# A two-layer FNet and PEER kernel: score weights made from two pieces of w_q at a time, and four smaller moves of buffers and order

## The chip, the cores and the metric

The kernel runs on one core of one Trainium2 chip. The metric is the device time of one execution in microseconds (us); a run's number is the time of that core. Five engines work side by side, each with its own instruction stream: PE (matrix multiply; PEld is its weight load), DVE (elementwise work and reductions), ACT (activations and copies), POOL (here one power per tile) and SP, whose stream issues the DMAs. The engines meet only at semaphores.

## The reference

The input x has 2048 rows of 512 numbers. Two sublayers alternate, twice each, and each adds its result to x:

```python
def A(x):                       # Fourier mixing, real part
    a, b = x @ dft_hid_re.T, x @ dft_hid_im.T
    return dft_seq_re @ a - dft_seq_im @ b
def B(x):                       # PEER: 32 heads, 16 + 16 keys, 256 experts, top 2 of the pairs
    q = einsum("nd,dhc->nhc", x, w_q)            # w_q: 512 x 32 x 256
    s1, s2 = q[..., :128] @ k1.T, q[..., 128:] @ k2.T      # 16 scores each
    ... top 2 of s1, top 2 of s2, top 2 of their four sums, softmax g ...
    act = gelu(einsum("nd,nhkd->nhk", x, u[top_e]))
    return einsum("nhk,nhk,nhkd->nd", g, act, v[top_e])
x = x + A(layernorm(x)); x = x + B(layernorm(x))
x = x + A(layernorm(x)); x = x + B(layernorm(x))
```

## The kernel before

**Numbers in two parts.** Every operand of a large matmul is split into a high part (rounded to the PE's fp32r) and a low part (the rest): xh and xl for the normalized x, ch and cl for a piece C of the sequence DFT matrix, dh and dl for the hidden DFT, wh and wl for the scores. A product is three matmuls: high by high, high by low, low by high.

**Setup.** w_q is never multiplied by x. The scores are linear in x, so k1 and k2 are first multiplied into w_q, which gives wh and wl (512 x 2 x 32 x 16). w_q comes in 32 loads of 512 KB (two heads each, tile wr). For each one DVE splits it into three bf16 pieces (line 381, f1, and line 384, f2, tile w), PE does 24 small matmuls of 48 columns against the keys (line 392, f3), DVE adds up the three pieces (line 397, f4, tile ws), ACT writes wh (line 404) and DVE wl (line 407). One such group on PE is called a visit here. The hidden DFT, u and v come through wr too and are split (lines 324 to 332).

**Sequence DFT.** `seq_unit` does the sequence DFT of one block of 256 rows (the last 256 rows: two of 128): for each of 16 row tiles s of x a piece C is loaded (line 454, tile raw, four buffers), ACT rounds it to ch (line 458), DVE makes cl (line 462), and PE adds 12 matmuls of 512 columns into four PSUM accumulators acc (line 518; lines 498 and 503 for the first s tiles). ACT and DVE then take acc out as pth and ptl (lines 543 and 546).

**Row tiles.** `token_tile` takes 128 rows through the rest: the second (hidden) DFT on pth and ptl (line 615, f), the addition of x (line 625), layer norm (lines 245 to 263, 271), a transpose (line 664), scores (lines 694 and 698, copied by ACT to tile sc, line 703), the product with u (line 725) and its gelu on act (lines 730 to 745), the top-2 chain on DVE (lines 778 to 894), a transpose of the choice (lines 903 and 907, tile qt), one-hot masks on DVE (lines 926 and 932, tile lr), mask matmuls (line 943), the copy of their diagonal by ACT (line 955), which goes out to DRAM and back as gt (line 999 and after), the weights times act (line 1014), a transpose (line 1023, then ph and pl, lines 1027 and 1031), the product with v (lines 1044 and 1048) and the addition to x (line 1064). The very last row tile, called fine, takes the diagonal by matmuls (line 978, weighed at line 1012) instead of the DRAM way.

**The order.** Every step is an `Op` with an engine, a planned cost, what it comes after, what buffers (`Hold`) it takes and gives back, and a priority. `Plan.run` places all of them once, by planned costs, when the kernel is built; each engine then executes its stream strictly in that order. `behind` is a constraint on the order alone. Buffers are counted in `BUFS`. While PE waits for the first data it runs ten matmuls without use (`FILL0`), and others are put in planned gaps at the end.

**The start.** x comes in 16 loads of 256 KB (line 297), the C pieces between them. For the first `FIRST` tiles ACT makes xh straight from x and a second full-precision copy for xl (both line 271), and the PE work of one tile is f (8 matmuls with xh) and g (4 with xl).

The buffers and the diagonal's copy as they stand:

```python
BUFS = {"acc": 4, "bank": 4, "raw": 4, "c": 3, "p": 1, "row": 4, "wr": 5, "wp": 2,
        "tok": 3, "sc": 1, ..., "lr": 4, ...}
...
hgs, hbs = Hold("p" if spare_p else "sc"), [Hold("bank") for _ in range(2)]
...
t["gs"] = work([P, 16, 4, E], F32, "sc") if not spare_p else mixed()...
```

Of the kernel before, what the change touches and what calls it, by code (L numbers as in the profile page):

```python
# [8 lines left out]
F32 = mybir.dt.float32  # L9
# [15 lines left out]
SP = 1  # L25
# [19 lines left out]
FIRST = 4  # L45
# [115 lines left out]
def load(kb):  # L161
    return kb / 256 * 1.05
# [3 lines left out]
def spectral_peer_kernel(ctx: ExitStack, tc, x_in, cseq, ctile, dhid, wq, k1t, k2t, ut, vm, out):  # L166
# [9 lines left out]
    BUFS = {"acc": 4, "bank": 4, "raw": 4, "c": 3, "p": 1, "row": 4, "wr": 5, "wp": 2,  # L176
            "tok": 3, "sc": 1, "eq": 1, "act": 3, "q": 2, "top": 1, "qt": 1, "lr": 4, "gt": 1, "pp": 1, "gdr": 2, "bn": 1}
# [19 lines left out]
    half = const.tile([P, 1], F32, name="half")  # L197
    picks = const.tile([P, P], F32, name="picks")

# [40 lines left out]
    def ln_stats(get, i, after, prio):  # L240
        bn, h = {}, Hold("bn")

        def f0():
            bn[0] = apool.tile([P, 6], F32, name="bn", bufs=BUFS["bn"])
            nc.vector.bn_stats(bn[0], get())

        a = op("DVE", dve(512), f0, after, take=[h], prio=prio)
        return ln_rest(lambda: bn[0], h, i, [a], prio)

    def ln_rest(bn, h, i, after, prio):  # L250
# [14 lines left out]
        a = op("DVE", 0.1, f1, after, last=[h], prio=prio)  # L265
        a = op("DVE", 0.1, f2, [a], prio=prio)
        a = op("POOL", 0.5, f3, [a], prio=prio)
        return op("DVE", 0.1, f4, [a], prio=prio)
# [9 lines left out]
    def xhat(layer, i, get, after, take, last, prio):  # L278
        if layer == 0 and i < FIRST:
# [3 lines left out]
                                  [a], last=last, prio=prio)  # L283
# [6 lines left out]
    xload = {}  # L290
    for i in range(NT):
        def first(i=i):
            h, t = Hold("wr"), {}

            def f():
                t[0] = setup_pool().tile([P, D], F32, name="wr", bufs=BUFS["wr"])
                nc.sync.dma_start(t[0], x_in[i * P:(i + 1) * P, :])
# [3 lines left out]
            a = ln_stats(lambda: t[0], i, [a], prio)  # L301
            xhat(0, i, lambda: t[0], [a], [], [h], prio)
        first()
# [4 lines left out]
    def setup():  # L308
# [63 lines left out]

        for hf in range(2):
            for g in range(H // HG):
                prio = (3, hf, g)
                a0, hw, r0 = wr(wq[hf, g * HG:(g + 1) * HG].rearrange("h c d -> c h d"), prio, xload[NT - 1])
                hp, hb, t = Hold("wp"), Hold("bank"), {}

                def f1(r0=r0, t=t):
                    t[1] = setup_pool().tile([P, HG, D], F32, name="w1", bufs=BUFS["wp"])  # L380
                    nc.vector.tensor_sub(t[1], r0(), upper(r0()))  # L381

                def f2(t=t):
                    nc.vector.tensor_sub(halves(t[1], 0), t[1], upper(t[1]))  # L384

                def f3(hf=hf, r0=r0, t=t):
                    t[3] = bank([P, KD * HG, 64])
                    ws = (upper(r0()), upper(t[1]), halves(t[1], 0))
                    for k in range(KD):
                        for a in range(HG):  # L390
                            for n, w in enumerate(ws):
                                nc.tensor.matmul(t[3][:, k * HG + a, :3 * E], w[:, a, k * P:(k + 1) * P],
                                                 kb[hf], start=(n == 0), stop=(n == 2), skip_group_check=True)

                def f4(t=t):
                    t[4] = setup_pool().tile([P, KD, HG, E], F32, name="ws", bufs=BUFS["wp"])
                    nc.vector.tensor_reduce(t[4].rearrange("p k a e -> p (k a) e"),
                                            t[3][:, :, :3 * E].rearrange("p b (n e) -> p b e n", e=E),
                                            axis=AX.X, op=ALU.add)

                hs = slice(g * HG, (g + 1) * HG)

                def f5(hf=hf, hs=hs, t=t):
                    nc.scalar.copy(wh[:, :, hf, hs, :], t[4])

                def f6(hf=hf, hs=hs, t=t):
                    nc.vector.tensor_sub(wl[:, :, hf, hs, :], t[4], as32(wh[:, :, hf, hs, :]))

                a1 = op("DVE", dve(1024), f1, [a0], take=[hp], prio=prio)
                a2 = op("DVE", dve(1024), f2, [a1], prio=prio)  # L410
                a3 = op("PE", 24 * 0.0255 + 0.1, f3, [a2, kready[hf]], take=[hb], last=[hw], prio=(0, 0))
                a4 = op("DVE", dve(384), f4, [a3], last=[hb], prio=prio)
                a5 = op("ACT", act(128), f5, [a4], prio=prio)
                setup_done.append(op("DVE", dve(128), f6, [a5], last=[hp], prio=prio))
# [19 lines left out]
    def seq_unit(layer, at, n, banks="acc"):  # L434
# [10 lines left out]
        pieces = {}  # L445

        def piece(p):
# [18 lines left out]
            b1 = op("ACT", act(512), f1, [a], take=[hc], prio=(-1,) + turn)  # L466
            c1 = op("DVE", dve(512), f2, [b1], last=[hr], prio=(-1,) + turn)
# [14 lines left out]
        for s0 in range(0, NT, 2):  # L482
# [5 lines left out]
            if layer == 0 and at == 0 and s0 < FIRST:  # L488

                for s in (s0, s0 + 1):  # L490
                    ready, hc, moving = pieces[s]

                    def f(s=s, moving=moving, parts=(0, 1)):
                        for d in range(KD):
                            if s == 0:
# [695 lines left out]
```

## Time and profile before

| what | us |
|---|---|
| three runs, median (lowest to highest) | 1264.51 (1264.24 to 1266.38) |
| the profiled execution, whole | 1266.79 |
| its span, first to last instruction | 1264.9 |
| PE busy in the span | 1250.8 |
| DVE busy | 994.2 |
| ACT busy | 466.5 |
| first useful matmul | 6.62 after the start |

A line of the time order reads: start, duration, engine, line of the kernel, operation, output<-inputs, shape, count, and in brackets the idle time of that engine just before and what ended it. A line of the waits reads: who waited, for whom, us in total, times, longest. PE is busy nearly all the time, but its instructions overlap each other, so what counts is the step from one start to the next.

### The profile page before, as it was taken

How to read it: one execution, taken by the hardware profiler on the slowest of the kernel's cores; microseconds unless marked ns; L12 is line 12 of the kernel's file. 1: busy time of each engine (PE TensorE's matmuls, PEld its weight loads, DVE VectorE, ACT ScalarE, POOL GpSimd, SP SyncE). 2: the span in 40 equal slices, each digit the busy share in tenths (PEclk: the TensorE clock that was granted, in tenths of full speed). 3: DMA queues.
4: the chain of work that ended last, by engine and by line, in shares of the span. 5: the costliest groups of instructions: out<-in, count | busy, mean ns of one | idle time of the engine just before them, and what ended most of it. 6: DMA issues, size and time to landing. Idle time of an engine off the chain costs nothing.

```text
span 1264.9 us, 20684 instructions
## 1 busy us (share of the span) xinstructions
PE 1250.8 (99%) x7804; PEld 1036.8 (82%) x7804; DVE 994.2 (79%) x2257; ACT 466.5 (37%) x966; POOL 45.7 (4%) x71
## 2 busy tenths in 40 slices
PE   9999999999999999999999999999999999999998
PEld 6777778887888888899878887888888888888886
DVE  8899998988887957779884378695685847778598
ACT  7522243343433333333563333333332433333232
POOL 2010000000000000000000000000000000000000
PEclk9999999999999999999999999999999999999999
DMA  7866541333233241413455204314142331414201
GB/s 235 268 197 213 180 150 34 92 70 65 67 84 76 76 101 50 112 39 88 121 133 135 67 26 104 81 59 109 42 108 51 93 91 51 108 43 110 58 9 35
DMA packets 224101, 121.18 MB, mean 96 GB/s; under 512 B 136448, under 2 KB 202496, under 8 KB 224000
## 3 DMA queue, kind: packets, MB, share of 16 engines
q1 hardware_dynamic: 224000, 119.85, 35.4%
q8 instruction: 61, 1.00, 0.3%
q14 instruction: 40, 0.33, 0.1%
HBM read 107.36 MB, written 12.45 MB: 95 GB/s over the span
## 4 chain that ended last, share of the span: by engine, by line
PE 71%; DVE 16%; issue 6%; DMA 2%; ACT 2%; SPq 1%; POOL 1%; POOLq 0%; DVEq 0%; ACTq 0%
PE acc L518 39%; PE bank L615 11%; PE bank L694 7%; PE bank L698 4%; PE bank L725 3%; DVE cl L462 2%; DVE w L384 2%; PE bank L1044 2%; DVE w L381 2%; PE bank L518 1%; PE bank L943 1%; DVE eq L778 1%; PE bank L1048 1%; PE bank L664 1%; POOL stats L260 1%
## 5 line engine op out<-in xcount | busy, mean ns | idle before, releaser
L518 PE MATMUL acc<-ch,xh 128*128 128x512 f32 (+1 forms) x1072 | 407.9, 381 | 0.0
L518 PE MATMUL acc<-ch,xl 128*128 128x512 f32 (+1 forms) x1072 | 397.8, 371 | 0.3 <-DVE xl L287 0.3
L518 PE MATMUL acc<-cl,xh 128*128 128x512 f32 (+1 forms) x1072 | 397.8, 371 | 0.0
L458 ACT CAST ch<-raw 128x512 fp32r<-128x512 f32 x256 | 158.4, 619 | 263.7 <-PE acc L518 227.0
L462 DVE TENSOR_TENSOR cl<-raw,ch 128x512 fp32r<-128x512 f32 x256 | 175.5, 687 | 72.4 <-ACT ch L458 52.9
L518 PEld LDWEIGHTS acc<-cl,xh 128*128 128x128 f32 x1072 | 201.9, 188 | 35.2
L518 PEld LDWEIGHTS acc<-ch,xh 128*128 128x128 f32 x1072 | 202.1, 189 | 32.6 <-issue 1.4
L518 PEld LDWEIGHTS acc<-ch,xl 128*128 128x128 f32 x1072 | 202.5, 189 | 31.6 <-DVE xl L287 1.0
L615 PE MATMUL bank<-dh,pth 128*128 128x512 f32 (+1 forms) x264 | 102.9, 392 | 0.4 <-ACT pth L543 0.4
L694 PE MATMUL bank<-wh,tok 128*128 128x512 f32 x256 | 100.2, 392 | 1.3 <-ACT sc L955 1.0
L615 PE MATMUL bank<-dl,pth 128*128 128x512 f32 (+1 forms) x264 | 100.6, 383 | 0.0
L694 PE MATMUL bank<-wl,tok 128*128 128x512 f32 x256 | 99.7, 390 | 0.0
L615 PE MATMUL bank<-dh,ptl 128*128 128x512 f32 (+1 forms) x264 | 95.9, 384 | 0.0
L784 DVE TENSOR_TENSOR tmp<-sc 128x512 f32<-128x512 f32 (+1 forms) x66 | 44.4, 672 | 61.7 <-ACT sc L703 60.8
L926 DVE TENSOR_TENSOR lr<-iota,qt 128x1024 f16<-128x1024 f16 x124 | 80.6, 684 | 10.6 <-ACT qt L907 10.6
L260 POOL TENSOR_TENSOR stats<-stats,half 128x1 f32<-128x1 f32 x64 | 44.4, 697 | 1183.7 <-DVE stats L257 1182.5
L778 DVE TENSOR_TENSOR eq<-sc,val 128x1024 f16<-128x1024 f32 (+1 forms) x66 | 78.5, 1190 | 1.5
L703 ACT COPY sc<-bank 128x512 f32<-128x512 f32 x64 | 36.8, 589 | 104.1 <-PE bank L698 73.1
L698 PE MATMUL bank<-wh,tok 128*128 128x512 f32 x256 | 68.5, 389 | 0.0
L800 DVE TENSOR_TENSOR eq<-eq 128x256 f16<-128x256 f16 (+3 forms) x198 | 60.0, 303 | 1.6
L615 PEld LDWEIGHTS bank<-dh,pth 128*128 128x128 f32 x264 | 49.6, 188 | 10.4 <-ACT pth L543 0.9
L694 PEld LDWEIGHTS bank<-wh,tok 128*128 128x128 f32 x256 | 48.1, 188 | 11.6 <-ACT raw L271 1.1
(152 smaller groups left out, 1790.7 us busy)
## 6 DMA issues: line engine op xcount, KB each, us to landing
raw<-in_cseq SPq DMA_DIRECT2D x224, 256.0 KB, 2.8
wr<-in_wq SPq DMA_DIRECT2D x32, 512.0 KB, 4.1
raw<-in_ctile SPq DMA_DIRECT2D x32, 256.0 KB, 2.9
wr<-in_x SPq DMA_DIRECT2D x16, 256.0 KB, 3.4
row<-in_x SPq DMA_DIRECT2D x16, 256.0 KB, 3.1
x2d<-row SPq DMA_DIRECT2D x16, 256.0 KB, 2.0
row<-x2d SPq DMA_DIRECT2D x16, 256.0 KB, 3.2
out<-row SPq DMA_DIRECT2D x16, 256.0 KB, 2.3
```

Source lines behind the costliest of these rows:

```text
L260: nc.gpsimd.tensor_tensor(st[:, 1:2], st[:, 1:2], half, op=ALU.pow)
L458: nc.scalar.copy(t[1], t[0])
L462: nc.vector.tensor_sub(t[2], t[0], as32(t[1]))
L518: nc.tensor.matmul(target(d), w[:, s, d * P:(d + 1) * P], moving(s % per, part), start=(s == 0 and k == 0 and d % blocks == 0), stop=(s == ...
L615: nc.tensor.matmul(t["y", cs.start], w[:, k, c, t0:t0 + P], r[:, c, k, cs], start=(z == 0 and c == 0 and m == 0), stop=(z == len(steps) - ...
L694: nc.tensor.matmul(t["pc", hf], t["th"][:, k, :], r[:, k, hf], start=(k == 0 and r is wh), stop=False)
L698: nc.tensor.matmul(t["pc", hf], t["tl"][:, k, :], wh[:, k, hf], start=False, stop=(k == KD - 1))
L725: nc.tensor.matmul(t["xu"], w[:, k, :], r[:, k, :], start=(m == 0), stop=(m == 3 * KD - 1))
L778: nc.vector.tensor_tensor(t["eq"][:, :, cols], flat("sc")[:, :, cols], val(rank_, cols), op=ALU.is_equal)
L784: nc.vector.tensor_max(t["tmp"][:, :, cols], flat("sc")[:, :8, cols], flat("sc")[:, 8:, cols])
L800: nc.vector.tensor_max(s[:, :m], s[:, :m], s[:, m:2 * m])
L926: nc.vector.tensor_tensor(t["m", hf, r], io2, row_of(r, hf), op=ALU.is_equal)
```

## The change

Five things are changed.

1. **Two pieces of w_q per visit.** The split of two loads is done one after the other, then PE does both groups of 24 matmuls in one step (`PG = 2`), 16 visits instead of 32. ACT and DVE then write wh and wl for both at once (256 elements instead of 128). The planned cost of the second split step goes up by 0.136. Buffers wr: 4 instead of 5; w1: 3 and ws: 2 instead of two for both.
2. **x's load buffers in pairs.** Two x tiles share one wr buffer, so four buffers hold eight tiles; before, five held five.
3. **The diagonal's copy in the masks' buffer.** The four mask tiles lr become two of double size; gs, the diagonal's copy, is written over the first one and no longer takes sc.
4. **Second DFT tile by tile.** The matmuls of line 615 of a unit's second row tile come behind all those of its first.
5. **The start.** x's first tile comes in two halves, statistics by halves, and DVE makes its xh in two halves with (x - mean) * rstd. x's second tile is issued ahead of the first C piece. `FIRST` is 6, and the PE work of an early tile is in three groups (xh by ch, xh by cl, xl by ch), each with its own waits.

Besides, half lies in a spare column of picks, and a tile of 128 bytes a partition is put in as a gap. The core of the diff:

```diff
-FIRST = 4
+FIRST = 6
-    BUFS = {... "wr": 5, "wp": 2, ... "lr": 4, ...}
+    BUFS = {... "wr": 4, "w1": 3, "ws": 2, ... "lr": 2, ...}
...
+        cut = [slice(0, D // 2), slice(D // 2, D)]
+                nc.sync.dma_start(t[0][:, cs], x_in[:P, cs])
+        for z, cs in enumerate(cut):
+            a = xload[0] = op("SP", load(128), f_load(cs), take=[] if z else take, prio=(-2, 0, 0, z), lag=2.3)
+            stat.append(op("DVE", dve(D // 2), lambda ...: nc.vector.bn_stats(t[1][:, z], t[0][:, cs]), [a], ...))
+        a, b = ln_rest(..., hb, 0, stat, (-3, 0))
+        for cs in cut:
+            xhigh[0].append(op("DVE", 0.3, lambda cs=cs: nc.vector.tensor_scalar(
+                xh[:, 0, cs], t[0][:, cs], stats[:, 0, 0:1], stats[:, 0, 1:2], op0=ALU.subtract, op1=ALU.mult), [b], prio=(-4, 0)))
...
-            a = xload[i] = op("SP", load(256), f, take=[h], prio=(-2, i, 0), lag=2.3)
-            prio = (-2 if i < 8 else 0, i)
+            a = xload[i] = op("SP", load(256), f, take=take, prio=(-2, i, 0) if i > 1 else (-2, 0, 0, 2), lag=2.3)
+            prio = (-5 if i == 1 else -2 if i < 8 else 0, i)
...
+        PG = 2
         for hf in range(2):
-            for g in range(H // HG):
+            for g in range(0, H // HG, PG):
+                for m in range(PG):
+                    a1 = op("DVE", dve(1024), f1, [a0], take=hp[m:], prio=prio + (m,))
+                    split.append(op("DVE", dve(1024) + 0.136, f2, [a1], prio=prio + (m,)))
-                a3 = op("PE", 24 * 0.0255 + 0.1, f3, [a2, kready[hf]], take=[hb], last=[hw], prio=(0, 0))
+                a3 = op("PE", PG * 24 * 0.0255 + 0.23, f3, split + [kready[hf]], take=hb, last=hw + hp, prio=(0, 0))
-                a5 = op("ACT", act(128), f5, [a4], prio=prio)
-                setup_done.append(op("DVE", dve(128), f6, [a5], last=[hp], prio=prio))
+                a5 = op("ACT", act(128 * PG), f5, sums, prio=prio)
+                setup_done.append(op("DVE", dve(128 * PG), f6, [a5], last=[hws], prio=prio))
...
-                       take=[hb] if z == 0 else [], behind=[a_row],
+                       take=[hb] if z == 0 else [],
+                       behind=[a_row] + ([hidden[n]] if n in hidden and at < len(units) - 1 else []),
+            hidden[n] = a
...
+                        if hf == 0:
+                            t["mm", r] = work([P, 2, 16, E, 4], F16, "lr")
+                        t["m", hf, r] = t["mm", r][:, hf]
-        hgs, hbs = Hold("p" if spare_p else "sc"), [Hold("bank") for _ in range(2)]
+        hgs, hbs = Hold("p") if spare_p else hls[0], [Hold("bank") for _ in range(2)]
-                    t["gs"] = work([P, 16, 4, E], F32, "sc") if not spare_p else mixed()...
+                    m = mixed() if spare_p else t["mm", 0].rearrange("p f g e t -> p (f g e t)").bitcast(F32)
+                    t["gs"] = m.rearrange("p (g t e) -> p g t e", t=4, e=E)
```

How the streams move at three places. The changed kernel's line numbers are its own: 319 and 342 load x, 325 and 330 are the halves' statistics and xh, 441 and 444 are the split (before 381 and 384), 464 the sum (397), 474 wl (407), 518, 522 and 526 the C piece (454, 458, 462), 1004 and 1013 the masks (926 and 932), 1050 the fine tile's evacuation (969), 1093 and 1095 the weighing (1012 and 1014), 814 and 817 the gelu's products (742 and 745), 1114 pl (1031).

The start of SP's stream and of DVE's (the number behind a name is that of the buffer's tile), before:

```order
L297 DMA wr_98<-in_x 128x512
L454 DMA raw_100<-in_cseq 128x2x256
L297 DMA wr_102<-in_x 128x512
L454 DMA raw_104<-in_cseq 128x2x256
L297 DMA wr_109<-in_x 128x512
```

```order
L245 BN_STATS bn<-wr 128x6
L254 BN_AGGR stats<-bn 128x2
L257 TENSOR_SCALAR stats<-stats 128x1
L462 TENSOR_TENSOR cl<-raw,ch 128x512
L263 SCALAR_TENSOR_TENSOR stats<-stats 128x1
```

The same two, after:

```order
L319 DMA wr_97<-in_x 128x256 x2
L342 DMA wr_97<-in_x 128x512
L518 DMA raw_102<-in_cseq 128x2x256
L518 DMA raw_105<-in_cseq 128x2x256
L342 DMA wr_110<-in_x 128x512
```

```order
L325 BN_STATS bn<-wr 128x6 x2
L254 BN_AGGR stats<-bn 128x2
L257 TENSOR_SCALAR stats<-stats 128x1
L245 BN_STATS bn<-wr 128x6
L330 TENSOR_SCALAR xh<-wr,stats 128x256
L254 BN_AGGR stats<-bn 128x2
L330 TENSOR_SCALAR xh<-wr,stats 128x256
L257 TENSOR_SCALAR stats<-stats 128x1
L263 SCALAR_TENSOR_TENSOR stats<-stats 128x1
L526 TENSOR_TENSOR cl<-raw,ch 128x512
```

The first C piece moves from the second place of SP's stream to the fourth, and on DVE the second tile's statistics (line 245) now stand between the first tile's statistics and its xh.

DVE's stream in the middle of the w_q stage, before, one visit (w_1058 is the split piece) up to the next one's first step:

```order
L381 TENSOR_TENSOR w_1058<-wr 128x1024
L397 TENSOR_REDUCE ws<-bank 128x128
L384 TENSOR_TENSOR w_1058<-w_1058 128x1024
L462 TENSOR_TENSOR cl<-raw,ch 128x512
L407 TENSOR_TENSOR wl<-ws,wh 128x4x32
L381 TENSOR_TENSOR w_1110<-wr 128x1024
```

And after, from the end of the first piece of a visit (w_944; w_1015 is its second) to the first piece of the next visit (w_1045):

```order
L444 TENSOR_TENSOR w_944<-w_944 128x1024
L464 TENSOR_REDUCE ws<-bank 128x4x32 x2
L441 TENSOR_TENSOR w_1015<-wr 128x1024
L526 TENSOR_TENSOR cl<-raw,ch 128x512
L474 TENSOR_TENSOR wl<-ws,wh 128x4x64
L444 TENSOR_TENSOR w_1015<-w_1015 128x1024
L441 TENSOR_TENSOR w_1045<-wr 128x1024
```

Two pieces are now split in a row for one visit, with the C pieces' cl among them. The sums of one visit come between the two pieces of the next, and wl is one operation for two pieces.

The end of DVE's stream, from the fine tile's last mask to its weighing (act and bank), before:

```order
L932 TENSOR_TENSOR cl<-cl,raw 128x1024
L969 TENSOR_TENSOR pth<-bank,picks 128x64x8 x2
L1064 TENSOR_TENSOR row<-row,bank 128x512
L1031 TENSOR_TENSOR pl<-bank,ph 128x256
L742 TENSOR_TENSOR act<-act 128x256
L745 TENSOR_TENSOR act<-act 128x256
L1012 TENSOR_TENSOR act<-act,bank 128x256
```

And after:

```order
L1013 TENSOR_TENSOR cl<-cl,raw 128x1024
L1050 TENSOR_TENSOR pth<-bank,picks 128x64x8 x2
L1114 TENSOR_TENSOR pl<-bank,ph 128x256
L817 TENSOR_TENSOR act<-act 128x256
L1093 TENSOR_TENSOR act<-act,bank 128x256
```

An addition to x has left this stretch (it stands further ahead, just before the fine tile's top-2 chain), and the gelu's first product (line 742, now 814) comes ahead of the masks. A pl that stood between the fine tile's masks has also gone ahead of its top-2 chain.

More of the change, by code (lines that the diff above doesn't have):

```diff
@@ L173, in spectral_peer_kernel @@
     ctx.enter_context(tc.manual_schedule())
-    BUFS = {"acc": 4, "bank": 4, "raw": 4, "c": 3, "p": 1, "row": 4, "wr": 5, "wp": 2,
-            "tok": 3, "sc": 1, "eq": 1, "act": 3, "q": 2, "top": 1, "qt": 1, "lr": 4, "gt": 1, "pp": 1, "gdr": 2, "bn": 1}
+    BUFS = {"acc": 4, "bank": 4, "raw": 4, "c": 3, "p": 1, "row": 4, "wr": 4, "w1": 3, "ws": 2,
+            "tok": 3, "sc": 1, "eq": 1, "act": 3, "q": 2, "top": 1, "qt": 1, "lr": 2, "gt": 1, "pp": 1, "gdr": 2, "bn": 1}
     plan = Plan(BUFS)
@@ new lines, in setup, with f4 @@
+                a3 = op("PE", PG * 24 * 0.0255 + 0.23, f3, split + [kready[hf]], take=hb, last=hw + hp, prio=(0, 0))
+                for m in range(PG):
+                    def f4(m=m, t=t):
+                        if m == 0:
+                            t["ws"] = setup_pool().tile([P, KD, PG, HG, E], F32, name="ws", bufs=BUFS["ws"])
+                        nc.vector.tensor_reduce(t["ws"][:, :, m],
+                                                t["b", m][:, :, :3 * E].rearrange("p (k a) (n e) -> p k a e n", e=E, a=HG),
+                                                axis=AX.X, op=ALU.add)
+                    sums.append(op("DVE", dve(384), f4, [a3], behind=sums, take=[] if m else [hws], last=hb[m:m + 1], prio=prio))
@@ L465, in piece @@
                    prio=(0,) + turn if layer or at else (-2, p, 1))
-            b1 = op("ACT", act(512), f1, [a], take=[hc], prio=(-1,) + turn)
-            c1 = op("DVE", dve(512), f2, [b1], last=[hr], prio=(-1,) + turn)
+            b1 = high[p] = op("ACT", act(512), f1, [a], take=[hc], prio=(-1,) + turn)
+            c1 = op("DVE", dve(512), f2, [b1], last=[hr], prio=(-1,) + turn,
+                    behind=xhigh[0] + [xvar[1]] if layer == 0 and at == 0 and p == 0 else [])
             def moving(q, part):
@@ L491, in seq_unit @@
                     ready, hc, moving = pieces[s]
-                    def f(s=s, moving=moving, parts=(0, 1)):
-                        for d in range(KD):
-                            if s == 0:
-                                acc[d] = psum.tile([P, 2, T], F32, name=banks, bufs=BUFS[banks])
-                            for part in parts:
-                                nc.tensor.matmul(target(d), xh[:, s, d * P:(d + 1) * P], moving(0, part),
-                                                 start=(s == 0 and part == 0), stop=False, skip_group_check=True)
@@ L501, in g, with f @@
-                    def g(s=s, moving=moving):
-                        for d in range(KD):
-                            nc.tensor.matmul(target(d), xl[:, s, d * P:(d + 1) * P], moving(0, 0),
-                                             start=False, stop=False, skip_group_check=True)
-                    seq_last = op("PE", 2 * KD * MM512, f, [ready, xhigh[s], seq_last], take=hold if s == 0 else [], prio=rank)
-                    seq_last = xfree[s] = op("PE", KD * MM512, g, [xready[layer, s], seq_last], last=[hc], prio=rank)
+                    def f(ds, w, part, s=s, moving=moving):
+                        def f():
+                            for d in ds:
+                                if s == 0 and w is xh and part == 0:
+                                    acc[d] = psum.tile([P, 2, T], F32, name=banks, bufs=BUFS[banks])
+                                nc.tensor.matmul(target(d), w[:, s, d * P:(d + 1) * P], moving(0, part),
+                                                 start=(s == 0 and w is xh and part == 0), stop=False,
+                                                 skip_group_check=True)
+                        return f
@@ L915, in row_of @@
             return m[:, :, None, :].to_broadcast([P, 16, E, 4])
-        made, hls = [], []
+        made, first_m, hls = [], [], [Hold("lr") for _ in range(2)] if not fine else []
+        spare_p = fine or layer and at == len(units) - 2 and i == tiles_of(n)[-1]
         soon = (0, 1, -1, i) if layer and at == len(units) - 2 else prio
```

141 lines of the change are left out of this document (93 added, 48 removed).

## Prediction

> **What bounds the kernel now.** I read the page's first part, then busy time by stretches, then every place where PE waits.
>
> ```profile
> span 1264.9 us, 20684 instructions
> PE 1250.8 (99%) x7804; PEld 1036.8 (82%) x7804; DVE 994.2 (79%) x2257; ACT 466.5 (37%) x966; POOL 45.7 (4%) x71
> ```
>
> ```profile
> 6.60:45.00 38.40, 38.38 (x168) 31.51 (x169) 35.12 (x101) 31.59 (x49) 9.50 (x15) 1.00 0.77 239
> 45.00:185.00 140.00, 138.10 (x1260) 109.83 (x1260) 135.43 (x197) 37.68 (x78) 5.86 (x4) 1.00 0.64 203
> 1230.00:1265.00 35.00, 29.77 (x247) 22.37 (x246) 28.01 (x85) 8.24 (x21) 0.00 (x0) 0.99 0.18 35
> ```
>
> The columns are the stretch, its length, then busy us of PE, PEld, DVE, ACT, POOL, and the granted clock. PE is the bound from 6.6 us on, at full clock, and the change takes no work from it: the two instruction streams hold the same useful matmuls, and one matmul without use fewer. So only PE's small waits can be won: the start, the w_q stage (45 to 185, where DVE too is busy for 135.4 of 140 us), single waits in the middle, and the last 35 us, where one row tile goes from engine to engine.
>
> **Fewer visits.** PE and PEld around one visit:
>
> ```profile
> 90.28 0.20 PE L392 MATMUL bank<-kb,wr 128*128 128x48 bf16 x1
> 90.31 0.45 PE L392 MATMUL bank<-kb,w 128*128 128x48 bf16 x2
> 90.56 0.10 PEld L392 LDWEIGHTS <-w 128*128 128x128 bf16 x1 [0.17 <-DVE w L384]
> 91.13 0.47 PE L518 MATMUL acc<-ch,xh 128*128 128x512 f32 x1
> 91.44 0.39 PE L518 MATMUL acc<-ch,xl 128*128 128x512 f32 x1
> 91.67 0.39 PE L518 MATMUL acc<-cl,xh 128*128 128x512 f32 x1
> ```
>
> The first large matmul after the small ones takes a step of 0.31 (91.13 to 91.44), the next 0.23. So each visit costs 0.08 beyond its own work, and there are 16 fewer: -1.3 us. Both steps are in the trace, so the bounds are near, -1.6 to -1.0.
>
> **The wait for the split.** In the rows above the third small matmul stands until 90.56, 0.25 after the second, because the third bf16 piece (line 384) is late. DVE in the same stretch:
>
> ```profile
> 87.50 1.25 DVE L381 TENSOR_TENSOR w<-wr 128x1024 f32<-128x1024 f32 x1
> 88.63 0.59 DVE L397 TENSOR_REDUCE ws<-bank 128x128 f32<-128x384 f32 x1
> 89.10 1.41 DVE L384 TENSOR_TENSOR w<-w 128x1024 bf16<-128x1024 f32 x1
> 90.37 0.71 DVE L462 TENSOR_TENSOR cl<-raw,ch 128x512 fp32r<-128x512 f32 x1
> 90.96 0.32 DVE L407 TENSOR_TENSOR wl<-ws,wh 128x128 fp32r<-128x128 f32 x1
> 91.17 1.25 DVE L381 TENSOR_TENSOR w<-wr 128x1024 f32<-128x1024 f32 x1
> ```
>
> From start to start a visit costs DVE 3.67 (1.13, 0.47, 1.27, 0.59, 0.21). PE needs 12 steps of 0.23, 24 of about 0.025 and the 0.08: 3.4. The difference, 0.26, is the wait: with 12 large matmuls to a visit DVE is the bound. In the waits of this stage PEld stands at line 392 for:
>
> ```profile
> PEld L392 <- DVE w L384: 2.6, 11, 0.6
> PEld L392 <- DMA raw<-in_cseq: 0.8, 3, 0.3
> PEld L392 <- DMA wr<-in_wq: 0.5, 2, 0.3
> ```
>
> Together 3.9 us in 16 of 32 visits. In the changed stream, between the second and the seventh double visit, PE has 138 large matmuls and five visits of 48: 138 x 0.23 (31.5) + 5 x 1.28 (6.4) = 37.9. DVE has 10 splits (24.0), 10 sums (4.7), 5 double wl (0.21 and 0.13 more for the second 128 elements, an estimate from the 1.13 of 1024: 1.7), 12 cl (7.1) and small ones (0.2): 37.7. So the stage comes from 0.26 short per visit to balance. Half the wl operations save DVE a little besides. I leave 1.0 us of waits, because balance is no slack and 16 joints remain, and win 2.9. Bounds: all 3.9 gone, or all of them kept since DVE still has nothing to spare: -3.9 to 0.
>
> The Trainium skill, "Perfetto Trace Analysis", section "Optimization Strategy", says that the same gap repeating on the engine that should be saturated can mean that too few buffers are left for the next tile. The trace disagrees for 11 of the 16 gaps, whose releaser is DVE's line 384; only 2 of them (0.5 us) end with a w_q load. By the rule the change would make the gaps longer, since four wr buffers now go out and back two at a time; that is the slower rival below, and the sum by it is 1268 instead of 1258.
>
> **The start.** What sets the first matmul:
>
> ```profile
> 0.74 0.39 SPq L297 DMA_DIRECT2D wr<-in_x  x1
> 1.18 0.42 SPq L454 DMA_DIRECT2D raw<-in_cseq  x1
> 1.65 0.46 SPq L297 DMA_DIRECT2D wr<-in_x  x1
> 2.15 0.43 SPq L454 DMA_DIRECT2D raw<-in_cseq  x1
> 3.59 0.69 DVE L245 BATCH_NORM_STATS2 bn<-wr 128x6 f32<-128x512 f32 x1 [1.33 <-DMA wr<-in_x]
> 4.30 0.62 ACT L458 CAST ch<-raw 128x512 fp32r<-128x512 f32 x1 [2.29 <-DMA raw<-in_cseq]
> 6.22 0.69 DVE L245 BATCH_NORM_STATS2 bn<-wr 128x6 f32<-128x512 f32 x1 [0.50 <-DMA wr<-in_x]
> 6.62 0.50 PE L498 MATMUL acc<-ch,xh 128*128 128x512 f32 x1 [0.86 <-ACT xh L271]
> ```
>
> The first load is there 2.85 after its issue (0.74 to 3.59), the second 3.1, the third 4.6 (1.65 to 6.22). Now the first C piece is fourth, at about 2.15, and x's second tile third, and DVE reads that tile's statistics before it makes the first xh. If both come as fast as the first load did, C is there at 5.0, ch at 5.6, and x's tile at 4.5, so that xh starts after its 0.69, at 5.2, and takes under 0.4: first matmul 5.6, 1.0 earlier. If both take what the third load took, C comes at 6.75 and ch at 7.4, 0.8 later. Two of the loads ahead are half as large, which speaks for less than 4.6, but it is the row of the nearest place in the queue: I take 6.8, +0.2, and keep -1.0 to +0.8. After that the second tile needs 12 steps of PE (2.7 us) before it is wanted, and its statistics now run earlier than before, so PE should not stand there. The two tiles more that ACT copies twice cost it about 0.4 us, hidden in the 38.4 us where it is busy for 31.6; the extra loads in flight from sharing wr win nothing, since PE is busy for 38.38 of these 38.40 us. The spare column and the gap move no work.
>
> **The middle.** Waits of PE, PEld and ACT from 185 to 1184:
>
> ```profile
> PE bank L1023 <- DVE act L1014: 2.0, 4, 0.8
> PE bank L694 <- ACT sc L955: 1.0, 1, 1.0
> PEld bank L725 <- ACT sc L955: 0.7, 1, 0.7
> ACT sc L955 <- DVE eq L778: 36.1, 14, 6.1
> ```
>
> ACT stands for 36.1 us until DVE's chain gives sc back, with everything behind it in its stream (ch, xh, the other copies). The copy now goes into a buffer that is free, so this wait ends, and with it the two waits of PE that it caused: -1.7. What comes next there is lr: the next tile's masks wait until the copy has gone out, but they stand a whole top-2 chain later than sc did. The second DFT tile by tile changes the order of equal matmuls and costs nothing by itself. The 2.0 us at line 1023 hang on the way through DRAM; they may shrink when the copy is earlier, or come back elsewhere, since the whole order is new: -3.7 to +2.0.
>
> **The end.** After the masks of the fine tile:
>
> ```profile
> 1250.81 0.42 DVE L1031 TENSOR_TENSOR pl<-bank,ph 128x256 fp32r<-128x256 f32 x1
> 1255.50 0.68 DVE L1064 TENSOR_TENSOR row<-row,bank 128x512 f32<-128x512 f32 x1
> 1256.43 0.41 DVE L742 TENSOR_TENSOR act<-act 128x256 f32<-128x256 f32 x1
> 1257.33 0.42 ACT L744 ACTIVATE act<-act 128x256 f32<-128x256 f32 x1
> 1257.78 0.42 DVE L745 TENSOR_TENSOR act<-act 128x256 f32<-128x256 f32 x1 [0.93 <-ACT act L744]
> 1258.31 0.42 DVE L1012 TENSOR_TENSOR act<-act,bank 128x256 f32<-128x256 f32 x1
> ```
>
> The pl at 1250.81 (0.33 by its step) leaves the masks. The weighing at 1258.31 waits for the gelu, whose first product came at 1256.43; that now stands ahead of the masks, and the weighing would start some 0.5 earlier. Against that the addition (0.6 by its step) now stands before the top-2 chain, where DVE may or may not be free. I take -0.6, bounds -1.2 to +0.6.
>
> **The sum.** +0.2 - 1.3 - 2.9 - 1.7 - 0.6 = -6.3 us. The profiled span of 1264.9 becomes 1258.6. That execution took 1266.8 in all, 2.3 above the runs' median of 1264.5, so I put the same 6.3 on the median: 1258.2, said as 1258. A difference of 0.2% (2.5 us) is about what a measurement of this kernel can tell from none.
>
> **The rivals.**
> - *It trades waits for waits.* DVE stays short by as much in the w_q stage, the middle gets as many new waits as it loses, C lands late. Then -1.3 - 0.6 + 0.8 and perhaps 0.5 of the split: about -1.6, 1263. For it: DVE is busy for 135.4 of 140 us, and the whole order is new. Against: the counts above balance, and the wait for sc has a cause that is gone.
> - *Slower: w_q arrives late.* Both buffers of a visit come free at its end. The visit after next needs the first of them when DVE has done the one between: a period of 37.9 / 5 = 7.6 less the visit's 1.3 and about 0.3 of lead, 6.0 us later. A load of w_q takes in this stage
>
> ```profile
> DMA to landing us min/median/max: 3.6/4.0/5.8
> ```
>
>   and is issued some 0.4 after the release. It becomes the bound from 6.0 on, and outweighs the gain when the 13 visits after the first three are each 0.7 late. At 0.8 late: +10.4 - 6.3, 1268.6. Against it: even the worst row gives 6.2, so nearly every load would have to be slower than the slowest.
> - *All goes well.* C lands early (-1.0), no split wait is left (-3.9), the four waits at line 1023 go too (-3.7), -1.3, -1.2: -11.1, 1253.4. For it: an ACT that is not stopped gives back a margin everywhere. Against: five good ends at once.
>
> **How the numbers follow.** The forecast has 0.69, with 1254.5 to 1261.5 as its own range; waits for waits 0.17; w_q late 0.06; all well 0.08. The range 1253.0 to 1263.8 takes in the first two and half of the last. Faster than by 0.2% (under 1262) are the forecast and the last, 0.77; the same, 0.17; slower, 0.06.
>
> **What would show it.** Line 456 (392 before) waiting in few of 16 visits, and DVE's waits for wr near none: right for the stage; a repeated wait of DVE on w_q loads: the slower rival. The first matmul of line 563 between 5.6 and 7.4. No wait of ACT's line 1036 on the top-2 chain, and no new large wait of DVE's line 1004 on the copies out. The weighing (line 1093) right after the picking matmuls. I would be wrong if PE's waits in the w_q stage stayed near 3.9 us, or if the middle showed new waits of several us.

## The result and the profile after

The changed kernel takes 1257.97 us (median of 4 runs, 1257.36 to 1258.65) against 1264.55 for the kernel before: ratio 0.9944, 95% interval 0.9933 to 0.9956 (the two medians alone give 0.9948). Forecast were 1258.0 and 6.3 us less; 6.6 less were measured. The sum came out; three of its terms did not, as the experiments show.

The page's first part, after:

```profile
span 1256.0 us, 20620 instructions
PE 1245.7 (99%) x7803; PEld 1037.3 (83%) x7803; DVE 993.5 (79%) x2244; ACT 461.5 (37%) x949; POOL 47.2 (4%) x71
```

Busy time by the same stretches (the last one moved with the end):

```profile
6.41:45.00 38.59, 38.23 (x166) 31.01 (x166) 35.23 (x101) 31.43 (x48) 9.81 (x15) 1.00 0.79 252
45.00:185.00 140.00, 139.21 (x1283) 113.99 (x1281) 136.17 (x182) 37.66 (x68) 4.21 (x4) 1.00 0.62 203
1221.00:1256.00 35.00, 29.34 (x244) 22.25 (x242) 26.89 (x81) 7.24 (x19) 0.40 (x1) 1.00 0.14 31
```

PE did 23 matmuls more between 45 and 185 us. Its waits in that stretch (who waited, for whom: us in total, times, longest), where before PEld had stood 11 times for DVE's split:

```profile
PEld bank L684 <- DVE ptl L614: 1.4, 2, 0.9
PEld L456 <- DVE w L444: 0.5, 2, 0.2
PEld L456 <- DMA wr<-in_wq: 0.3, 1, 0.3
```

The middle, 185 to 1184 us, the same view:

```profile
ACT sc L775 <- DVE eq L850: 65.2, 15, 8.0
ACT lr L1036 <- PE bank L1024: 13.8, 17, 2.0
PE acc L586 <- DVE ptl L614: 0.7, 2, 0.5
```

The diagonal's copy (line 1036) waits for PE's own result instead of DVE's top-2 chain, and PE's own waits at the weights' transposes, the scores and the u products (2.0, 1.0 and, on PEld, 0.7 us in the rows of before) are gone but for one of 0.3 on PEld at the u products. But ACT stands no less: its copy of the scores (line 775, before 703) now waits 65.2 us for the chain, where before the two copies waited 36.1 and this:

```profile
ACT sc L703 <- DVE eq L778: 16.3, 8, 7.2
```

The start, in order of time:

```profile
2.11 0.95 SPq L518 DMA_DIRECT2D raw<-in_cseq  x2
4.98 0.69 DVE L245 BATCH_NORM_STATS2 bn<-wr 128x6 f32<-128x512 f32 x1 [0.46 <-DMA wr<-in_x]
5.74 0.62 ACT L522 CAST ch<-raw 128x512 fp32r<-128x512 f32 x1 [3.72 <-DMA raw<-in_cseq]
6.41 1.46 PE L563 MATMUL acc<-ch,xh 128*128 128x512 f32 x4
12.66 0.72 PE L563 MATMUL acc<-ch,xh 128*128 128x512 f32 x2 [0.26 <-ACT xh L274]
```

C was there 3.6 us after its issue (2.11 to 5.74), between the 2.85 and 4.6 of the two cases in the prediction. The end, after and then before:

```profile
1213.78 0.38 PE L684 MATMUL bank<-dh,pth 128*128 128x256 f32 x1 [0.45 <-ACT pth L611]
1220.31 0.68 DVE L1004 TENSOR_TENSOR lr<-iota,qt 128x1024 f16<-128x1024 f16 x1
1220.47 0.93 POOL L260 TENSOR_TENSOR stats<-stats,picks 128x1 f32<-128x1 f32 x1 [42.18 <-DVE stats L257]
1221.43 0.16 DVE L263 SCALAR_TENSOR_TENSOR stats<-stats 128x1 f32<-128x1 f32 x1 [0.44 <-POOL stats L260]
1240.37 0.22 DVE L942 TENSOR_TENSOR q<-key,df 128x128 f16<-128x128 f16 x1
1245.27 1.31 DVE L1050 TENSOR_TENSOR pth<-bank,picks 128x512 f32<-128x512 f32 x2
1248.81 0.42 DVE L1093 TENSOR_TENSOR act<-act,bank 128x256 f32<-128x256 f32 x1 [1.57 <-PE bank L1059]
1249.75 0.38 PE L1104 MATMUL bank<-identf,act 128*128 128x128 f32 x2
1252.28 0.69 DVE L1147 TENSOR_TENSOR row<-row,bank 128x512 f32<-128x512 f32 x1 [0.69 <-PE bank L1131]
```

```profile
1222.92 0.38 PE L615 MATMUL bank<-dh,pth 128*128 128x256 f32 x1 [0.45 <-ACT pth L543]
1229.41 0.56 POOL L260 TENSOR_TENSOR stats<-stats,half 128x1 f32<-128x1 f32 x1 [45.40 <-DVE stats L257]
1249.04 0.22 DVE L870 TENSOR_TENSOR q<-key,df 128x128 f16<-128x128 f16 x1
1254.28 1.31 DVE L969 TENSOR_TENSOR pth<-bank,picks 128x512 f32<-128x512 f32 x2
1258.78 0.44 PE L1023 MATMUL bank<-identf,act 128*128 128x128 f32 x2
1261.37 0.69 DVE L1064 TENSOR_TENSOR row<-row,bank 128x512 f32<-128x512 f32 x1 [0.69 <-PE bank L1048]
```

The first row of each is the last tile's first DFT matmul behind its last wait for pth. From there to the last addition it is 38.50 after (1213.78 to 1252.28) and 38.45 before (1222.92 to 1261.37).

**Where the time went, by stage.** For one number per stage I took, from each trace, every step from one PE matmul's start to the next, and subtracted the step that its shape has when nothing waits (0.2265 for 512 columns, 0.120 for 256, 0.108 for a transpose, 0.025 for the small ones of w_q, and so on). Without the matmuls of no use that is 1201.7 us of work in every kernel here. What is left is PE's lost time, and stages are cut where PE has done 40, 180 and 1170 us of work. Work and losses add up to the span (changed: 1201.74 + 7.81 + 5.92 + 16.77 + 23.72 = 1255.96). Each ratio is to the kernel before as it ran beside that kernel; its median there was 1264.55 for the changed kernel and 1265.10 to 1265.33 for the others, so up to 0.8 us of a difference between two medians of this table is not the edit's.

| kernel | median us | ratio to before, interval | lost: to 40 | w_q, 40 to 180 | middle, to 1170 | last |
|---|---|---|---|---|---|---|
| before | 1264.55 | | 7.6 | 9.4 | 22.5 | 23.6 |
| b_again (before, second trace) | 1266.06, one run | | 7.8 | 9.3 | 21.9 | 23.6 |
| changed | 1257.97 | 0.9944 (0.9933 to 0.9956) | 7.8 | 5.9 | 16.8 | 23.7 |
| b_price | 1271.54 | 1.0050 (1.0037 to 1.0062) | 7.1 | 5.6 | 31.3 | 23.6 |
| a_noprice | 1261.28 | 0.9969 (0.9957 to 0.9981) | 7.9 | 7.1 | 18.2 | 24.0 |
| a_pg1 | 1260.77 | 0.9967 (0.9955 to 0.9980) | 8.2 | 6.3 | 18.8 | 23.9 |
| b_gs | 1273.06 | 1.0065 (1.0052 to 1.0077) | 6.9 | 9.5 | 20.0 | 33.9 |
| b_price_gs | 1272.86 | 1.0062 (1.0049 to 1.0074) | 7.0 | 6.2 | 22.4 | 33.9 |
| a_gs_sc | 1270.31 | 1.0046 (1.0034 to 1.0059) | 7.8 | 5.7 | 31.0 | 24.1 |
| a_cfirst | 1257.45 | 0.9938 (0.9924 to 0.9951) | 8.3 | 5.7 | 17.4 | 23.7 |
| a_nohid | 1269.13 | 1.0029 (1.0019 to 1.0040) | 7.3 | 6.1 | 18.2 | 34.0 |
| b_gs_hid | 1262.86 | 0.9979 (0.9970 to 0.9987) | 8.3 | 8.9 | 18.8 | 23.8 |
| b_price_gs_hid | 1261.09 | 0.9964 (0.9951 to 0.9978) | 6.9 | 6.1 | 19.8 | 23.8 |
| a_tail2 | 1257.31 | 0.9932 (0.9920 to 0.9945) | 8.0 | 5.7 | 16.6 | 22.8 |

So nothing came from the start (+0.2) or the end (+0.1), 3.5 us from the w_q stage and 5.8 (5.1 against the second trace) from the middle.

### The profile page after: what moved, and what is told of

The parts are those of the page before. It is cut to its first block, busy times and chain, and to the rows that moved or that the text cites. A ratio compares the mean times of both kernels' runs of the same rounds, so it can differ in the third digit from the quotient of the medians.

```text
span 1256.0 us, 20620 instructions
## 1 busy us (share of the span) xinstructions
PE 1245.7 (99%) x7803; PEld 1037.3 (83%) x7803; DVE 993.5 (79%) x2244; ACT 461.5 (37%) x949; POOL 47.2 (4%) x71
## 4 chain that ended last, share of the span: by engine, by line
PE 80%; issue 3%; DVE 2%; ACT 0%; POOLq 0%; POOL 0%; DVEq 0%
PE acc L586 43%; PE bank L684 12%; PE bank L766 9%; PE bank L770 4%; PE bank L797 3%; PE bank L1127 2%; PE bank L586 2%; PE bank L1024 1%; PE bank L736 1%; PE bank L1131 1%; PE bank L1104 1%; PE bank L975 0%; DVE eq L850 0%; PE bank L1059 0%; DVE eq L872 0%
## 5 line engine op out<-in xcount | busy, mean ns | idle before, releaser
L586 PE MATMUL acc<-ch,xh 128*128 128x512 f32 (+1 forms) x1064 | 403.8, 380 | 0.7 <-DVE ptl L614 0.7
L260 POOL TENSOR_TENSOR stats<-stats,picks 128x1 f32<-128x1 f32 x64 | 45.9, 719 | 1173.6 <-DVE stats L257 1167.8
L614 DVE TENSOR_TENSOR ptl<-acc,pth 128x512 fp32r<-128x512 f32 x62 | 42.3, 685 | 25.9 <-ACT pth L611 25.7
L684 PEld LDWEIGHTS bank<-dh,ptl 128*128 128x128 f32 x264 | 48.6, 188 | 11.3 <-DVE ptl L614 1.4
```

What stands on the lines that cost most here:

```text
L260: nc.gpsimd.tensor_tensor(st[:, 1:2], st[:, 1:2], half, op=ALU.pow)
L586: nc.tensor.matmul(target(d), w[:, s, d * P:(d + 1) * P], moving(s % per, part), start=(s == 0 and k == 0 and d % blocks == 0), stop=(s == ...
L614: nc.vector.tensor_sub(view(1, k, ds), acc[k], as32(view(0, k, ds)))
L684: nc.tensor.matmul(t["y", cs.start], w[:, k, c, t0:t0 + P], r[:, c, k, cs], start=(z == 0 and c == 0 and m == 0), stop=(z == len(steps) - ...
```

## The experiments

Names with b_ are the kernel before with something added, with a_ the changed kernel with something taken back. Between two such kernels the whole planned order can differ, so single microseconds of a stage are not all the work of the edit.

**A second trace of before.** No edit. 

> The kernel before, unchanged, profiled a second time. Its first profiled execution took 1266.8 us, 2.3 above the median of its runs; the changed kernel's took 1257.7, at its median, so 9.0 us of lost PE time between the two traces stand against 6.6 between the medians. If the four waits of PE for the weights times act (2.6 us at its line 1023) belong to the kernel, they are here again and the span is near 1264.9. If they were chance of that one execution, some 2 us of them are gone, the span is near 1262.5, and the rest of the middle and the 3.9 us at the split are unchanged.

The span was 1264.3. The four waits at line 1023 were there again, shorter (1.6 instead of 2.7 us between PE's starts), and the stages kept their losses to 0.7 us. They belong to the kernel. Why the two profiled executions lie 2.3 and 1.0 us above the median of the runs beside them stays open.

**The price of the split alone, in before.**

```diff
-                a2 = op("DVE", dve(1024), f2, [a1], prio=prio)
+                a2 = op("DVE", dve(1024) + 0.136, f2, [a1], prio=prio)
```

> The kernel before with one number changed: the second step of the split is planned 0.136 us dearer, as in the changed kernel. Theory one, joining the visits removes the wait for the split: PE still waits about 3.9 us at line 392 in half of 32 visits, 1264 us. Theory two, the plan's price removes it: the plan of before put a visit every 3.4 us of PE work although DVE needs 3.67, and with the true price it puts more matmuls between two visits; then at most 1 us of waits is left at line 392, and the time is 1261 to 1262.

Theory two, for the stage: its loss falls from 9.4 to 5.6 with single visits, and the view of PE's and PEld's waits, which before showed 11 for line 384, shows none. But in all neither theory held: the kernel is 6.4 us slower than before on that chip (1265.10), since the middle loses 9 more. Two stretches of it, and the longest wait there:

```profile
264.00:274.00 10.00, 8.16 (x63) 6.26 (x63) 9.31 (x19) 4.62 (x10) 0.00 (x0) 0.94 0.35 72
274.00:284.00 10.00, 6.79 (x21) 5.04 (x20) 9.57 (x27) 2.34 (x4) 1.07 (x2) 0.72 0.17 53
```

```profile
PE bank L664 <- ACT tok L271: 3.2, 1, 3.2
```

DVE is busy for 9.6 of 10 us and PE for 6.8, at a clock of 0.72: a jam of row tiles behind DVE's chain.

**The price taken out of the changed kernel.**

```diff
-                    split.append(op("DVE", dve(1024) + 0.136, f2, [a1], prio=prio + (m,)))
+                    split.append(op("DVE", dve(1024), f2, [a1], prio=prio + (m,)))
```

> The changed kernel without the 0.136 us in the planned cost of the split; visits stay joined in pairs. Theory one (joining): waits at line 456 stay under 1.2 us, 1258 us. Theory two (price): PE is offered a visit before its pieces are split, waits of 0.5 us in most of 16 visits, together 3 us or more, 1260.5 us.

Theory two: joined visits with the cheap price wait again, and the time is 3.3 us up. Of the 3.0 us more that PE loses in this trace, 1.2 lie in the w_q stage and 1.4 in the middle.

```profile
PEld L456 <- DVE w L444: 2.9, 8, 0.6
PE bank L456 <- DVE w L444: 2.0, 6, 0.5
```

**Single visits in the changed kernel.**

```diff
-        PG = 2
+        PG = 1
-                a3 = op("PE", PG * 24 * 0.0255 + 0.23, f3, ...
+                a3 = op("PE", PG * 24 * 0.0255 + 0.1, f3, ...
```

> The changed kernel with single visits (PG = 1, planned PE cost of a visit 0.71 as before); the dearer planned split and all else stay. Theory one (joining): the waits come back, 3 to 4 us, and 16 more steps of 0.08 (1.3 us): 1262 to 1263. Theory two (price): the waits stay near 1 us, only the 1.3 us of steps come back: 1259.3.

Theory two again for the waits:

```profile
PEld L456 <- DVE w L444: 0.5, 2, 0.4
```

The stage itself is only 0.4 worse than with joined visits. The stage's loss in the kernels that have or lack the two things, by where PE's step is too long:

| w_q stage, us lost | first large matmul after a visit | inside the visits | elsewhere | all |
|---|---|---|---|---|
| before (single, old price) | 2.9 | 5.0 | 1.5 | 9.4 |
| b_price (single, new price) | 2.9 | 0.7 | 2.0 | 5.6 |
| a_noprice (joined, old price) | 1.4 | 3.7 | 2.0 | 7.1 |
| changed (joined, new price) | 1.5 | 0.9 | 3.5 | 5.9 |
| a_pg1 (single, new price) | 2.8 | 1.2 | 2.3 | 6.3 |

Joining halves the first column, as forecast; the second, the wait for the split, goes with the price. With the old price joined visits (a_noprice) still lose 3.7 us there, against 5.0 in before.

The other 2 us of a_pg1 lie in the middle, in single waits (1.3 for ptl at 286 us, 0.9 at the masks' matmuls at 225) that the joined order does not have.

**The diagonal in the masks' buffer alone, in before** (part three of the change as its diff shows, with lr at two double buffers). 

> The kernel before with the third part of the change alone: the diagonal's copy goes over the first mask tile (two lr of double size) and no longer takes sc. Theory one (the wait for sc is what the middle loses): ACT no longer waits for the top-2 chain at its copy, PE's lost time from the w_q stage to the last tiles falls from 22 us to 17 to 20, the w_q stage keeps its 9.3 us: 1261 to 1263. Theory two (the middle's gain is the other order that comes with the new prices and visits): the middle stays near 22 us, 1264 to 1266.

The middle behaved by theory one (20.0), the total by neither: the last stage lost 10 us more, and the kernel is slower than before by 8. What the 10 us are is shown further down, where the two DFT tiles are put side by side.

**Price and diagonal together, in before.** 

> The kernel before with both: the split planned 0.136 us dearer, and the diagonal's copy in the masks' buffer. The dearer split alone took 3.7 us of lost time from the w_q stage and put 9.4 us into the middle, most of it between 239 and 283 us, where ACT waits to copy scores into sc and PE stands so long that its clock falls to half. Theory one (that jam is the one buffer sc, shared by scores and diagonal): the middle falls to 17 to 19 us with the w_q stage at 5.6, 1258.5 to 1260.5, most of the changed kernel's gain without joined visits. Theory two (the jam comes from the row tiles that start later): at least 5 of the 9.4 us stay, 1266 or more.

The jam is mostly gone (31.3 to 22.4), so most of it was the shared sc; 22.4 is still above the 17 to 19 of theory one. The last stage has the same 10 us on top, which neither theory had.

**The diagonal back in sc, in the changed kernel.**

```diff
-        hgs, hbs = Hold("p") if spare_p else hls[0], [Hold("bank") for _ in range(2)]
+        hgs, hbs = Hold("p" if spare_p else "sc"), [Hold("bank") for _ in range(2)]
-                    m = mixed() if spare_p else t["mm", 0]...
-                    t["gs"] = m.rearrange("p (g t e) -> p g t e", t=4, e=E)
+                    t["gs"] = work([P, 16, 4, E], F32, "sc") if not spare_p else mixed()...
...
-                           [pe[hf]] + evac, take=[hgs] if spare_p and not hf else [], last=hbs[hf:hf + 1], prio=prio))
+                           [pe[hf]] + evac, take=[] if hf else [hgs], last=hbs[hf:hf + 1], prio=prio))
```

> The changed kernel with the diagonal's copy back in sc (its masks stay in two double buffers). Theory one (the wait for sc): the middle loses 3 to 9 us more than the 16.8 of the changed kernel, with waits of PE behind ACT's copies, 1261 to 1267. Theory two (order): within 1 us of the changed kernel, 1257 to 1259.

Theory one, and more than it said: 12.3 us. The jam is there again, in the same place (264 to 294 us), with the old wait:

```profile
ACT sc L1036 <- DVE eq L850: 35.3, 17, 8.4
PE bank L736 <- ACT tok L274: 2.9, 2, 2.8
```

The true price thus pays only where sc is free, and the sc part is worth far more under that price (14.2 us of middle: 31.0 against 16.8) than in the order of before (22.5 against 20.0).

**The first C piece ahead again.**

```diff
-            a = xload[i] = op("SP", load(256), f, take=take, prio=(-2, i, 0) if i > 1 else (-2, 0, 0, 2), lag=2.3)
-            prio = (-5 if i == 1 else -2 if i < 8 else 0, i)
+            a = xload[i] = op("SP", load(256), f, take=take, prio=(-2, i, 0), lag=2.3)
+            prio = (-2 if i < 8 else 0, i)
-    xready[0, 0].behind.append(xvar[1])
...
-                    behind=xhigh[0] + [xvar[1]] if layer == 0 and at == 0 and p == 0 else [])
+                    behind=xhigh[0] if layer == 0 and at == 0 and p == 0 else [])
```

> The changed kernel with its first C piece ahead of x's second tile again, and without that tile's early statistics (the halves of the first tile stay). If the load order costs what the prediction put down (+0.2), the first useful matmul comes 0.2 earlier than the changed kernel's 6.41, and the time falls by as much, 1257.5 to 1258.2. If the gain of the order is in the second tile, PE waits for that tile after its first 12 matmuls by 0.5 us or more, and the time is 1258.5 to 1259.

Both things happened: the first matmul came at 5.92, and PE then stood 1.65 for the second tile's xh at 9.2. By the trace the loss to 40 us is 0.5 larger (8.3 against 7.8); by the runs (1257.45) nothing is to be told apart. The 5.92 alone says little: a_nohid, with the changed order of loads, also started at 5.92.

**The DFT's two tiles side by side again.**

```diff
-                       behind=[a_row] + ([hidden[n]] if n in hidden and at < len(units) - 1 else []),
+                       behind=[a_row],
```

> The changed kernel without the fourth part: the second DFT of a unit's two tiles is again interleaved. The prediction put this part at nothing. Theory one (it is what lets the diagonal lie in the masks' buffer): with the two tiles side by side, the second one's masks wait until the first one's copies have left the two double buffers, as in the kernel before with the third part alone, whose last stage lost 10 us; so the last stage loses about 34 us instead of 23.7: 1266 to 1270. Theory two (equal matmuls in another order cost nothing): 1257 to 1259.

Theory one by its numbers: 11 us up, and the last stage loses 34.0. DVE's stream at the end:

```profile
1241.13 0.21 DVE L942 TENSOR_TENSOR q<-key,df 128x128 f16<-128x128 f16 x1
1248.03 1.29 DVE L1004 TENSOR_TENSOR lr<-iota,qt 128x1024 f16<-128x1024 f16 x2
1260.34 0.42 DVE L1095 TENSOR_TENSOR act<-act,raw 128x256 f32<-128x256 f32 x1 [4.75 <-DMA raw<-gdr]
```

The masks of the tile before (lr, the last of them at 1248.03) now stand behind the fine tile's whole top-2 chain (its end: 1241.13); its diagonal then goes out to DRAM and back alone, and DVE waits 4.75 us for it with nothing else left. In the changed kernel these masks are made from 1220 on.

But the mechanism that theory one names is not what the trace shows. The masks' buffers were long free: the copies of the tile ahead had landed in DRAM at 1214.1 (at 1209.7 in the changed kernel). What came late is the choice q, from which the masks are made. PE transposes it (line 975) either ahead of the fine tile's own transposes (line 736) or behind that tile's transposes, scores and u products. Here, and then in the changed kernel:

```profile
1223.02 0.82 PE L736 MATMUL bank<-identf,tok 128*128 128x128 f32 x4 [0.27 <-ACT tok L274]
1223.54 0.22 DVE L942 TENSOR_TENSOR q<-key,df 128x128 f16<-128x128 f16 x1
1230.95 0.34 PE L975 MATMUL bank<-ident,q 128*128 128x128 f16 x3
```

```profile
1217.88 0.22 DVE L942 TENSOR_TENSOR q<-key,df 128x128 f16<-128x128 f16 x1
1218.90 0.33 PE L975 MATMUL bank<-ident,q 128*128 128x128 f16 x3
1222.28 0.90 PE L736 MATMUL bank<-identf,tok 128*128 128x128 f32 x4 [0.65 <-ACT tok L274]
```

Counted from the fine tile's DFT matmul behind its last wait for pth, DVE ends this chain (q) 8.6 us later here, in b_gs and in b_price_gs, 4.1 later in the changed kernel and 7.2 later in before, where PE could still transpose q 0.5 us ahead of the fine tile. In b_gs and here the weighing, the pl and the addition of the tile ahead (1.3 us of steps) stand before q on DVE; in before they stand behind it. So 1.5 us on DVE miss a turn on PE, and the three kernels that miss it are the three whose last stage loses 34.

**Parts three and four in before.** 

> The kernel before with parts three and four only: the diagonal in the masks' buffer and the second DFT tile by tile. If the 10 us that the third part alone lost at the end come from the two tiles side by side, the last stage is back near 23.7 us, the middle is at 17 to 20 and the w_q stage at 9.4: 1260 to 1262.5. If they come from the two buffers alone, the last stage stays near 34: 1270 or more.

The first reading, 0.4 above its range: the last stage is back at 23.8, the middle at 18.8, the w_q stage nearly as before (8.9).

**The price and parts three and four in before.** 

> The kernel before with three things: the split planned 0.136 us dearer, the diagonal in the masks' buffer, the second DFT tile by tile; visits stay single, x's buffers and the start are those of before. If these three carry the gain, the w_q stage loses about 6 us, the middle 17 to 19, the last 23.7: 1257.5 to 1259.5. If joined visits are needed (16 steps of 0.08, or the waits), it is 2 us or more above the changed kernel: 1260 to 1262.

1261.09, inside the second reading's range: these three win 4.2 us on that chip (1265.33 before), of the changed kernel's 6.6 in its own runs. But it is not for the reason which that reading names, since the w_q stage is as good as with joined visits (6.1 against 5.9). What is missing is in the middle (19.8 against 16.8), and 2.1 of it are the two single waits of a_pg1, here at 286 and 224 us.

**A version with another end.** Three order constraints: the pl of the tile two ahead behind the fine tile's variance (line 257), the masks behind its line 263, and the four matmuls of line 1127 not held behind the picking.

```diff
...
+            ahead_pl[-2].behind.append(lnvar[i])
+            for m in ahead_m[-2:]:
+                m.behind.append(a)
...
-                ends[-2].behind.extend(back)
```

> The changed kernel with three places of the end put otherwise. In it POOL's power of the last tile took 0.93 instead of 0.55 us, beside a mask step of DVE, and DVE then stood 0.44; one pl stood ahead of that tile's statistics (0.33); and the last transpose waited 0.4 on PE behind four matmuls of the other tile. Here the pl comes behind the statistics, the masks behind the power, and the four matmuls where PE made matmuls without use. If those readings hold, POOL takes 0.55, the last stage goes from 23.7 to about 22.6, and the time falls by 1.1 us, to 1256.9. If the end hangs on the top-2 chain's start in another way (DVE full up to it), less than 0.4 is won.

```profile
1219.95 0.55 POOL L260 TENSOR_TENSOR stats<-stats,picks 128x1 f32<-128x1 f32 x1 [41.97 <-DVE stats L257]
1220.53 0.16 DVE L263 SCALAR_TENSOR_TENSOR stats<-stats 128x1 f32<-128x1 f32 x1 [0.34 <-POOL stats L260]
1247.93 0.42 DVE L1098 TENSOR_TENSOR act<-act,bank 128x256 f32<-128x256 f32 x1 [1.48 <-PE bank L1064]
1248.40 0.44 PE L1109 MATMUL bank<-identf,act 128*128 128x128 f32 x2
```

As read: POOL takes 0.55, the transpose follows the weighing after 0.47 instead of 0.94, and the last stage loses 22.8. It is the best of all kernels here (1257.31, ratio 0.9932), though its interval overlaps the changed kernel's.

## Why the prediction was right, point by point

- **The start, +0.2.** Right in size, but not by the step that was counted. To 40 us of work the six traces with the changed start lost 7.8 on average (7.3 to 8.2), the seven with the old one 7.4 (6.9 to 8.3). The +0.2 was put on the first matmul (6.8 against 6.62); it came at 6.5 on average (5.9 to 7.1) against 6.6 with the old start, and PE lost the 0.5 after it, where the prediction saw no wait. The spread is larger than the term.
- **Fewer visits, -1.3, and the split wait, -2.9.** 4.2 forecast, 3.5 measured (3.4 against the second trace), and the step that failed is the cause. The balance was counted in the changed order and put down to joining. The waits go with the planned price: 9.4 to 5.6 with single visits (b_price), and they come back without it with joined ones (a_noprice). The plan of before counted a split at 2.27 us of DVE (two steps of 1.136), where the trace has 2.40. The 16 steps are saved (1.4 measured) and the visits lose 4.1 less, but the stage loses 2.0 more elsewhere, 1.9 of it in waits for ptl that the sum did not have. That is why b_price_gs_hid, with single visits, is level (6.1 against 5.9).
- **The repeated gaps.** The reading by the trace, which put them down to DVE's line 384 and not to too few buffers, held: b_price has the buffers of before and no such wait.
- **The middle, -1.7.** The mechanism was right and the size wrong: 5.1 to 5.8, beyond the bound of 3.7. Parts three and four alone give 3.1 to 3.7 of it (b_gs_hid), the four transposes that wait included, which I had kept for the good case. The remaining 2 come only with the joined order (a_pg1 lacks them too); 1.2 of them are two single waits of b_gs_hid (0.9 at 222 and 0.35 at 659 us), and why the joined order is free of such waits stays open. An ACT that isn't stopped was wrong: it stands longer (65.2 against 52.4 us), but at the scores' copy, where but for one wait of 0.3 nothing of PE hung on it.
- **Tile by tile, "costs nothing by itself".** The largest miss, though it left no trace in the sum: part three without part four costs 10 us at the end (b_gs, a_nohid). I had looked only at what the reordered matmuls cost, not at when the chain of a unit's second tile would end: side by side, q comes 8.6 instead of 4.1 us after the fine tile's DFT, and misses its turn on PE.
- **The end, -0.6.** Measured +0.1. Both gains came: from the last q to the evacuation 4.90 instead of 5.24 (1240.37 to 1245.27, 1249.04 to 1254.28), and the weighing 3.54 after that instead of 4.03. They were given back at two places that I had not priced: POOL and the pl ahead of the statistics (the power ends 7.62 after the first DFT matmul of those rows instead of 7.05), and the transpose, which stands 0.52 on PE behind the other tile's four matmuls once the weighing is done (1249.23 to 1249.75; before 0.05). a_tail2 took both back.

That the total was right is in part luck, because errors of opposite sign met: 0.7 too much on the w_q stage and 0.7 on the end, 3.4 to 4.1 too little on the middle, and a pair of traces that differs by some 2 us more than the medians do. No rival came about. The slower one is far away: PE waited for w_q loads once, for 0.3 us, and DVE once, for 1.1. One number of that rival is wrong: 13 visits each 0.5 late would already eat the 6.3, not 0.7.

No run takes x's paired load buffers (part two) or the halves of x's first tile alone; what they are worth by themselves is not shown.

## What to carry to other kernels

Where a planner places the work, a price that is 0.13 us too low on an operation that repeats is a wait each time, and it is mended in the price; but a truer price also moves everything behind it, and may only pay once the next bottleneck (here one buffer, sc) is free. Test such parts together, since alone part three and the price were slower by 0.65 and 0.5% and together with part four faster by 0.36%. And cost a reordering by which result comes later and whose turn it then misses, not by the instructions alone: here 1.5 us on DVE became 10 us.

## What the hardware showed that I had not expected

**POOL stands while DVE reads two tiles of SBUF.** In the changed kernel's trace the power (line 260, one element per partition, 64 times) takes 0.547 to 0.552 us in all of the 32 cases in which no DVE operation with two SBUF inputs ran in its first half microsecond. Of the other 32, 21 took 0.59 to 2.13 us; in each of these the DVE operation had begun before the power and went on for at least 0.18 us beside it. The row at 1220.47 above is one of the slow ones: it ends 0.41 after the mask step beside it (1220.99), and a_tail2 has 0.55 with a pl there that reads a PSUM bank. In the 11 others, which took 0.55, it began after the power or ended within 0.12 us of its start. The Trainium skill, "SBUF — State Buffer", section "SBUF: two separate sides", says that VectorE and GpSimd share one port pair, held for a whole instruction by a DVE operation with two SBUF inputs; the trace agrees.

**After a jam PE ran at half its clock.** In b_price, PE had stood for 2.2 us between 269.3 and 271.6, and soon after the granted clock was 0.50 for 3 us. In a_gs_sc, whose jam lies at the same place, it was 0.50 for 10 us. First b_price, then a_gs_sc:

```profile
273.00:276.00 3.00, 3.00 (x8) 2.00 (x6) 3.00 (x6) 0.43 (x2) 0.00 (x0) 0.50 0.16 62
```

```profile
280.80:291.00 10.20, 8.10 (x20) 5.83 (x20) 8.61 (x28) 4.24 (x11) 0.55 (x1) 0.50 0.25 26
```

So a jam costs more than its waits. The Trainium skill, "Trainium Architecture — The Big Picture", section "What this means for kernel authors", gives PE two clocks, one half of the other, by recent activity; these rows agree.
